# Attention: the 64-row rests of projections, v and output groups as two 32-row matmuls beside the logits

## Chip, cores and metric

The kernel runs on one core of a Trainium2 chip. The metric is the device time of one execution in microseconds, and the median of several runs is compared. Three runs of the kernel before took 1173.2, 1173.43 and 1175.64 us. A profile shows one execution: what each engine (PE, its weight loads PEld, DVE, ACT, POOL, and SP, which issues DMAs) did at which time.

## Reference

Four layers over x of 2048 rows and 576 columns: attention, gated MLP, attention, gated MLP, each added to its input. Cut to the attention, which the change touches:

```python
def _A_ref(x, wqkv, wo):
    B, S, D = x.shape                 # 1, 2048, 576
    H = 32; Dh = D // H               # 18
    W, dil = (8, 2)                   # each row looks at itself and 7 earlier rows, two apart
    qkv = (x @ wqkv).reshape(B, S, 3, H, Dh).transpose(2, 0, 3, 1, 4)
    q, k, v = (qkv[0], qkv[1], qkv[2])
    ...
    logits = jnp.einsum('bhsd,bhswd->bhsw', q, kg) * Dh ** (-0.5)
    logits = jnp.where(mask[None, None, :, :], logits, -1000000000.0)
    attn = _softmax(logits, axis=-1)
    o = jnp.einsum('bhsw,bhswd->bhsd', attn, vg)
    return o.transpose(0, 2, 1, 3).reshape(B, S, D) @ wo
...
x = x + _A_ref(_layernorm(x, axis=-1), A_wqkv, A_wo)
x = x + _B_ref(_layernorm(x, axis=-1), B_w_in, B_w_sp, B_b_sp, B_w_out)
```

The last two lines run twice.

## The kernel before

The layers are numbered 0 to 3; 0 and 2 are attention (`layer_A`), 1 and 3 the MLP. Rows are stored with even rows first, so that the dilated window becomes a band of eight neighbours. The normalized input stands transposed in `xnT`: 576 columns are five chunks of 128 rows, and the fifth holds 64 real rows; its other half meets weights that are zero (`zero_right`, L290). Every group that contracts over 576 columns is therefore five matmuls, c = 0 to 4, each over 128 rows:

- `PG(d, qk, cc)` (L402): one projection block of q or k, 512 columns, into a PSUM bank `pp`; `evac` copies it into a staging tile `stg`. When all parts of a staging tile are there, DMAs spread its heads, of 18 rows each, over `QK`, where each head has its own 32 rows; the queues of SP and POOL take them in turns.
- `VW(t, hh)` (L391): v for one key tile and half of the heads, 288 columns, into `v_ext`; `evac` is a copy on DVE or on ACT, by its last argument.
- `WO(i, hh)` (L523): half of an output tile, 288 columns; DVE adds the layer's input (L533).

The attention goes over 17 query tiles (t), two halves of the heads each, so over 34 steps s = 2t + hf (`NST`). `L_mm(s)` (L444) makes the logits of a step: 16 matmuls over 32 rows, a head per row tile of PE. The row tiles are 0 to 3 (j in the code). The pair jp = 0 uses row tiles 0 and 1, the pair jp = 1 uses 2 and 3, and each pair writes its own PSUM tile of two banks (`H_tile`, two of them, so a step's tiles are free again when the exponentials of the step before have read them). `EXP(s)` (L458) has ACT take the exponential of the two tiles, `PV(s)` (L468) multiplies with v in 16 matmuls into `O_ps`, and DVE divides (L482, L483). Four further PSUM banks (`PT_tile`) go round among O_ps, projections, v and output groups.

The order of the work on all engines is written out by hand (`manual_schedule`, L363); each engine runs its own instructions in program order. The loop at L762 does for each step s: `L_mm(s + 1)`, `EXP(s + 1)`, `PV(s)`, and then what `table` lists for s:

- projections: twelve `PG`, one in each of steps 1 to 12 in layer 0, in twelve of steps 0 to 12 in layer 2;
- v groups: one in most steps from 14 in layer 0 and from 3 in layer 2, up to step 29; from step 14 on every second one is evacuated by ACT, in layer 2 all of those before;
- output groups from step 8, one in a step, two in step 18;
- the normalization of finished output tiles: `LN_STATS` (DVE, then epsilon and power on POOL, L231 and L232), a step later `LN_XN` (POOL, L252 and L255) and the store `XST` (SP), later `XN_ST` and `LN_T`; loads `XO` of the layer's input (SP).

The rows from 1024 on of `QK` come from the projections of these steps; the logits of step 16 are the first to read them, and those of step 17 the first to read what the last two blocks (d = 3, d = 4) bring.

```python
for s in range(NST):
    if s + 1 < NST:
        L_mm(s + 1)
        EXP(s + 1)
    PV(s)
    for f, a in table.pop(s, []):
        f(*a)
```

Of the kernel before, what the change touches and what calls it, by code (L numbers as in the profile page):

```python
# [18 lines left out]
P = 128  # L19
# [44 lines left out]
class K:  # L64
# [267 lines left out]
    def layer_A(self, li):  # L332
# [57 lines left out]

        def VW(t, hh, dve):  # L391
            nk = tdim(t)[0]
            pv = self.PT_tile([P, 512], f32, "pv")
            for c in range(5):
                nc.tensor.matmul(pv[:nk, 0:288], lhsT=self.xnT[:, c, k0_(t):k0_(t) + nk],  # L395
                                 rhs=wv_sb[:, c, hh * 288:(hh + 1) * 288], start=(c == 0), stop=(c == 4))
            evac(v_ext[:nk, t, 16 * hh:16 * hh + 16, 0:DH], pv[:nk, 0:288].rearrange("p (b d) -> p b d", d=DH), dve)
# [4 lines left out]
        def PG(d, qk, cc, dve, queues=(nc.sync, nc.gpsimd)):  # L402
# [11 lines left out]
            pp = self.PT_tile([P, 512], f32, "pp")  # L414
            w0 = d * P + (640 if qk else 0)
            for c in range(5):
                w = wqk[:, c, w0:w0 + P] if c < 4 else wqk4[:, w0:w0 + P]
                nc.tensor.matmul(pp[:, :], lhsT=w, rhs=self.xnT[:, c, cc * 512:(cc + 1) * 512],  # L418
                                 start=(c == 0), stop=(c == 4))
# [21 lines left out]
        NST = 2 * NT  # L441
        L_tiles = {}

        def L_mm(s):  # L444
            t, hf = divmod(s, 2)
            nk, nq = tdim(t)
            L_tiles[s] = [self.H_tile("L_ps") for _ in range(2)]
            for jp in range(2):
                for ftl in range(4):
                    g = 4 * hf + ftl  # L450
                    for jj in range(2):
                        j = 2 * jp + jj
                        nc.tensor.matmul(L_tiles[s][jp][:nk, jj, ftl * P:ftl * P + nq],  # L453
                                         lhsT=kT[32 * j:32 * j + 32, g, k0_(t):k0_(t) + nk],
                                         rhs=qT[32 * j:32 * j + 32, g, q0_(t):q0_(t) + nq],
                                         start=True, stop=True, tile_position=(32 * j, 0))

        def EXP(s):  # L458
            nk, nq = tdim(s // 2)
            for jp, L_ps in enumerate(L_tiles.pop(s)):  # L460
                Lv = L_ps[:].rearrange("p a (b c) -> p a b c", c=P)
                nc.scalar.activation(out=P_bufs[(2 * s + jp) % 4][:nk, :, :, 0:nq], in_=Lv[:nk, :, :, 0:nq], func=ACT.Exp,  # L462
                                     scale=scale)
# [4 lines left out]
        def PV(s):  # L468
            t, hf = divmod(s, 2)
            nk, nq = tdim(t)  # L470
            O_ps = self.PT_tile([P, 512], f32, "O_ps")
            for jp in range(2):
                for ftl in range(4):
                    for jj in range(2):
                        idx = 4 * ftl + 2 * jp + jj
                        nc.tensor.matmul(O_ps[:, idx * (DH + 1):(idx + 1) * (DH + 1)],  # L476
                                         lhsT=P_bufs[(2 * s + jp) % 4][:nk, jj, ftl, :],
                                         rhs=v_ext[:nk, t, 16 * hf + idx, :], start=True, stop=True)
# [25 lines left out]
        def O_T(t):  # L504
            nq = tdim(t)[1]
            pt = self.PT_tile([P, 5, P], bf16, "pt")
# [16 lines left out]
        def WO(i, hh):  # L523
# [4 lines left out]
            pw = self.PT_tile([P, 512], f32, "pw")  # L528
            for c in range(5):
                nc.tensor.matmul(pw[:, 0:288], lhsT=oT[:, c, r0:r0 + P], rhs=wo_sb[:, c, hh * 288:(hh + 1) * 288],  # L530
                                 start=(c == 0), stop=(c == 4))
            hs = slice(hh * 288, (hh + 1) * 288)
            nc.vector.tensor_tensor(out=st["x"][:, hs], in0=pw[:, 0:288], in1=st["xo"][:, hs], op=ALU.add)  # L533
# [20 lines left out]
        if li == 0:  # L554
# [72 lines left out]
            VW(0, 0, False)  # L627
            VW(0, 1, False)
            VW(1, 0, False)
# [6 lines left out]
            VW(1, 1, False)  # L636
# [4 lines left out]
            VW(2, 0, False)  # L641
            VW(2, 1, False)
# [17 lines left out]
            for k_, (d, cc) in enumerate(order):  # L660
                for qk in ((1, 0) if d < 4 else (0,)):
                    PG(d, qk, cc, False, (nc.gpsimd, nc.sync) if d in (0, 4) else q2)
                if k_ == 3:
                    VW(3, 0, False)
                    VW(3, 1, False)
# [5 lines left out]
        else:  # L671
            for k_, (d, cc) in enumerate([(d, cc) for d in range(5) for cc in range(2)]):
                for qk in ((1, 0) if d < 4 else (0,)):
                    PG(d, qk, cc, k_ == 0, (nc.gpsimd, nc.sync) if d == 0 else q2)
# [10 lines left out]
        for t in range(nvw0, nvw - (1 if li == 0 else 0)):  # L685
            for hh in range(2):
                VW(t, hh, li == 0)
# [11 lines left out]
        def at(s, f, *a):  # L699
            table.setdefault(s, []).append((f, a))  # L700
        pgs = [(d, qk, cc) for d, cc in ((0, 2), (1, 2), (2, 2), (0, 3), (1, 3), (2, 3), (3, 2), (3, 3), (4, 2), (4, 3))
# [3 lines left out]
        for k_, (d, qk, cc) in enumerate(pgs):  # L705
            at(1 + k_ if li == 0 else (k_ * PG_END) // len(pgs), PG, d, qk, cc, True)
        vws = [(t, hh) for t in range(nvw, NT) for hh in range(2)]
        if li == 0:
            at(0, VW, *vws[0], True)
            at(13, VW, *vws[1], True)  # L710
# [4 lines left out]
        for k_, (t, hh) in enumerate(vws):  # L715
            assert vsteps[k_] <= 2 * t - 2 + hh
            at(vsteps[k_], VW, t, hh, vsteps[k_] >= PG_END and k_ % 2 == 0)
# [8 lines left out]
        for i in range(NS):  # L726
# [3 lines left out]
            at(s, WO, i, 0)  # L730
            at(s1, WO, i, 1)
# [20 lines left out]
        for k_, (d, qk, cc) in enumerate(pre):  # L752
# [3 lines left out]
            PG(d, qk, cc, li > 0 or k_ < 4, q2)  # L756
            if li == 0 and k_ == 3:
                self.fill_window_rows(QK, 1)
        if li == 0:
            VW(nvw - 1, 0, False)  # L760
            VW(nvw - 1, 1, False)
        for s in range(NST):  # L762
            if s + 1 < NST:
                L_mm(s + 1)
                EXP(s + 1)
            PV(s)
            for f, a in table.pop(s, []):
                f(*a)
        for s in sorted(table):
            for f, a in table[s]:  # L770
# [376 lines left out]
```

## Time and profile before

| what | us |
|---|---|
| runs | 1173.2, 1173.43, 1175.64 |
| the profiled execution | 1174.15, its span 1172.3 |
| PE matmuls busy | 1156.2 (99% of the span) |
| first burst of logits in layer 0, in layer 2 | at 42.90, at 614.14 |
| last burst in layer 0, in layer 2 | at 120.07, at 698.03 |
| exponentials (L462) | 136, 972 ns each |
| projection matmuls (L418) | 379 ns each, 128x512 |
| v and output matmuls (L395, L530) | 285 and 286 ns each, 128x288 |
| logit matmuls (L453) | 213 ns each, 32 rows x 120 columns |
| copies of v on ACT (L389), on DVE (L387) | 405 and 452 ns each |
| LN_XN on POOL (L252) | 2307 ns each |

A matmul's duration contains the time through the array; matmuls overlap, so what a matmul costs PE is read from the distance of two starts. In a timeline line, the first number is the start in the span, the second how long the merged instructions last, "x16" how many they are; what stands in brackets is idle time of the engine before it and what ended it. "SPq" and POOL lines with DMA_DIRECT2D are issues of DMAs, not their transfers.

### The profile page before, as it was taken

Reading aid. Unit: us, or ns where it says so; the run is one execution under the profiler, and the core shown is the slowest. Engines: PE = TensorE matmul, PEld = TensorE weight load, DVE = VectorE, ACT = ScalarE, POOL = GpSimd, SP = SyncE. Lnnn points to the kernel's source line nnn. Section 1 sums busy time; section 2 is a strip of 40 time slices with the busy share of each in tenths; the row PEclk is TensorE's granted clock in tenths of the full one; section 3 lists DMA queues with packets and bytes.
Section 4 is the critical chain, followed back from the end, with each engine's and each line's share of the span. In section 5 each row is a group of like instructions: output and inputs, shape, how many; then the busy total and the mean of one; then the engine's idle time right before and its main releaser. Section 6 shows DMA issues by size and latency. Waiting matters only on the chain.

```text
span 1172.3 us, 19950 instructions
## 1 busy us (share of the span) xinstructions
PE 1156.2 (99%) x8161; PEld 618.8 (53%) x8258; DVE 552.6 (47%) x1137; ACT 339.5 (29%) x491; POOL 280.4 (24%) x412
## 2 busy tenths in 40 slices
PE   9999999999999999999999999999999999999998
PEld 5567544444444444457755774444444444444677
DVE  8678788333223322235545786863332223322321
ACT  5578555011110111102256884541011110111000
POOL 3769855000000000002153897540000000000000
DMA  8799895000000000059547797940000000001332
GB/s 197 192 172 246 185 230 114 23 12 12 12 11 2 12 12 1 18 170 277 159 98 115 204 236 194 236 85 1 12 12 12 12 12 1 12 1 46 110 106 74
DMA packets 182800, 106.44 MB, mean 91 GB/s; under 512 B 134938, under 2 KB 164042, under 8 KB 182709
## 3 DMA queue, kind: packets, MB, share of 16 engines
q1 hardware_dynamic: 170117, 84.54, 31.6%
q0 software_dynamic: 6240, 14.88, 4.6%
q10 hardware_dynamic: 6352, 5.75, 1.6%
q8 instruction: 64, 1.05, 0.4%
q14 instruction: 27, 0.22, 0.1%
HBM read 42.40 MB, written 21.77 MB: 55 GB/s over the span
## 4 chain that ended last, share of the span: by engine, by line
PE 94%; DMA 2%; issue 1%; ACT 1%; DVE 1%; POOL 1%; SPq 0%; DVEq 0%; ACTq 0%
PE pg L986 42%; PE po L1035 12%; PE pz L962 6%; PE pz1s L962 6%; PE pzs L838 6%; PE pz L838 6%; PE pp L418 5%; PE pw L530 3%; PE pv L395 3%; PE L_ps L453 3%; PE O_ps L476 2%; DMA wqk_sb<-in_A_wqkv_dram 1%; ACT P_sb L462 1%; DMA QK<-stg 1%; POOL QK L78 1%
## 5 line engine op out<-in xcount | busy, mean ns | idle before, releaser
L986 PE MATMUL pg<-Wq,Z 128*128 128x512 bf16 x2256 | 497.7, 379 | 2.5
L986 PEld LDWEIGHTS <-Z 128*128 128x128 bf16 x2304 | 225.4, 98 | 271.9
L990 DVE TENSOR_TENSOR g_tmp<-pg,ln_xn 128x512 f32<-128x512 f32 x144 | 99.7, 692 | 421.5 <-PE pg L986 421.5
L981 ACT ACTIVATE z1T<-pz 128x1024 bf16<-128x1024 f32 x36 | 34.9, 1021 | 500.2 <-PE pz L962 500.2
L78 POOL DMA_DIRECT2D wout<-in_B_w_out_dram x4 | 4.3, 1080 | 598.8 <-PE pg L986 598.8
L1035 PE MATMUL po<-wout,Z 128*128 128x288 bf16 x1152 | 141.4, 286 | 0.0
L462 ACT ACTIVATE P_sb<-L_ps 128x960 bf16<-128x960 f32 (+1 forms) x136 | 124.6, 972 | 32.7 <-PE L_ps L453 31.5
L1035 PEld LDWEIGHTS <-Z 128*128 128x128 bf16 x1152 | 112.7, 98 | 28.8
L838 PEld LDWEIGHTS <-xnT 128*128 128x128 bf16 (+1 forms) x800 | 68.0, 97 | 76.4 <-issue 11.5
L991 DVE TENSOR_TENSOR Z<-g_tmp,z1T 128x512 bf16<-128x512 f32 x144 | 99.7, 692 | 12.2
L887 DVE BATCH_NORM_STATS2 z_st<-zp 128x6 f32<-128x512 bf16 (+1 forms) x160 | 91.2, 617 | 10.7 <-ACT zp L885 10.5
L962 PEld LDWEIGHTS <-w 128*128 128x128 bf16 (+1 forms) x640 | 53.7, 97 | 74.0 <-issue 13.6
L418 PE MATMUL pp<-xnT,wqk_sb 128*128 128x512 bf16 x341 | 81.4, 379 | 1.5 <-DMA wqk_sb<-in_A_wqkv_dram 0.5
L252 POOL TENSOR_SCALAR ln_xn<-x_new,ln_mv,ln_rstd 128x576 bf16<-128x576 f32 x32 | 73.8, 2307 | 2.3
L1045 DVE TENSOR_TENSOR x_new<-po,xo 128x288 f32<-128x288 f32 (+1 forms) x64 | 28.8, 456 | 87.4 <-PE po L1035 83.4
L962 PE MATMUL pz<-xnT,w 128*128 128x512 bf16 (+1 forms) x314 | 66.2, 380 | 0.3
L962 PE MATMUL pz1s<-xnT,w 128*128 128x512 bf16 (+1 forms) x314 | 65.9, 379 | 0.5 <-issue 0.3
L838 PE MATMUL pzs<-win2a,xnT 128*128 128x512 bf16 (+1 forms) x234 | 58.6, 358 | 0.7 <-DVE x_new L533 0.4
L838 PE MATMUL pz<-win2a,xnT 128*128 128x512 bf16 (+1 forms) x234 | 58.5, 357 | 0.3
L78 POOL DMA_DIRECT2D QK<-stg x80 | 48.4, 610 | 38.3 <-DVE stg L387 18.2
L911 POOL TENSOR_SCALAR Z<-zp,z_mv,z_rstd 128x256 bf16<-128x256 bf16 x32 | 54.6, 1706 | 3.3
L885 ACT ACTIVATE zp<-pz 128x1024 bf16<-128x1024 f32 (+2 forms) x56 | 36.6, 720 | 61.7 <-PE pz L838 61.7
(108 smaller groups left out, 950.7 us busy)
## 6 DMA issues: line engine op xcount, KB each, us to landing
xres<-x_new SPq DMA_DIRECT2D x48, 288.0 KB
xo<-xres SPq DMA_DIRECT2D x32, 288.0 KB
wout<-in_B_w_out_dram POOLq DMA_DIRECT2D x4, 1296.0 KB, 7.7
xn_rows<-ln_xn SPq DMA_DIRECT2D x32, 160.0 KB
xo<-xres SPq DMA_DIRECT2D x8, 576.0 KB
w<-in_B_w_in_dram SPq DMA_DIRECT2D x16, 256.0 KB
QK<-stg POOLq DMA_DIRECT2D x52, 72.0 KB, 4.2
QK<-stg SPq DMA_DIRECT2D x42, 72.0 KB
```

What stands on the lines that cost most here:

```text
L78: return eng.dma_start(out=out, in_=in_)
L252: e.tensor_scalar(out=xn[:nrows, 0:D], in0=x_t[:nrows, :], scalar1=mv[:nrows, 0:1], scalar2=rstd[:nrows, 0:1], op0=ALU.subtract, op1=ALU.mult)
L418: nc.tensor.matmul(pp[:, :], lhsT=w, rhs=self.xnT[:, c, cc * 512:(cc + 1) * 512], start=(c == 0), stop=(c == 4))
L462: nc.scalar.activation(out=P_bufs[(2 * s + jp) % 4][:nk, :, :, 0:nq], in_=Lv[:nk, :, :, 0:nq], func=ACT.Exp, scale=scale)
L838: nc.tensor.matmul(out[:, o0:o0 + n], lhsT=self.xnT[r0:r1, c, r * P:(r + 1) * P], rhs=win2(c)[r0:r1, w0:w0 + n], start=start, stop=stop, t ...
L887: nc.vector.bn_stats(out=st[:, x // 512, :], in_=zp[:, x:x + min(512, w0 + n - x)])
L911: eng.tensor_scalar(out=Z[:, b0:b1, i, :], in0=zv[:, b0:b1, :], scalar1=mv[:, 0:1], scalar2=rstd[:, 0:1], op0=ALU.subtract, op1=ALU.mult)
L962: nc.tensor.matmul(outs[a_], lhsT=w1[r0:r1, c, sub * P:(sub + 1) * P], rhs=self.xnT[r0:r1, c, q * 512:(q + 1) * 512], start=start, stop=st ...
L986: nc.tensor.matmul(pg[:, :], lhsT=Z[:, jj, i, sub * P:(sub + 1) * P], rhs=Wq[q][:, i, :], start=(i == 0), stop=(i == NS - 1))
L990: nc.vector.tensor_tensor(out=tmp[:], in0=pg[:, :], in1=bsp[:, qs], op=ALU.add)
L991: nc.vector.tensor_tensor(out=uT(jj)[:, sub, qs], in0=tmp[:], in1=z1Ts[jj, sub][:, qs], op=ALU.mult)
L1035: nc.tensor.matmul(acc[hh], lhsT=u_rows(j, i), rhs=wouts[j // NJH][:, j % NJH, hh * 288:(hh + 1) * 288], start=(j == 0), stop=(j == NJ - 1))
```

## The change

A group becomes a `Unit`. `plain()` does the five matmuls as before. A unit that is listed `early` is spread over two bursts of logits instead: `begin()` multiplies the first 32 of the 64 rest rows in row tile 0, at the head of the burst that precedes the unit's step; `middle()` does the four full chunks in the unit's place in the step; `end()` multiplies the other 32 rows in row tile 1 between the two halves of the next burst; `done()` evacuates right after the first of the two exponentials of that burst. One unit in each of steps 0 to 31 of both layers is early, 64 in all; a second or third unit of a step stays plain. The pairs of row tiles of the logits become (1, 2) and (0, 3). The four PSUM banks are allocated once and handed out by `take` by a written-down guess of when each is free; a begun unit holds its bank until it is done.

```diff
+        NST = 2 * NT
+        banks, free, held, now = [], [0.0] * 4, set(), [-1]
+        tails_w = []
+        JP = ((1, 2), (0, 3))
+
+        def take(name, rel=0.0):
+            if now[0] < 0:
+                return self.PT_tile([P, 512], f32, name), None
+            k_ = min((x for x in range(4) if x not in held), key=lambda x: free[x])
+            if rel is None:
+                held.add(k_)
+            else:
+                free[k_] = now[0] + rel
+            return banks[k_], k_
+
+        def mm(out, lr, start, stop, rg=None):
+            kw = {} if rg is None else dict(tile_position=(32 * rg, 0))
+            return nc.tensor.matmul(out, lhsT=lr[0], rhs=lr[1], start=start, stop=stop, **kw)
+
+        class Unit:
...
+            def plain(u):
+                ps, _ = take(u.name, 1.25)
+                for c in range(5):
+                    mm(ps[:, 0:u.n], u.op(c), c == 0, c == 4)
+                u.fin(ps)
+
+            def done(u):
+                held.discard(u.k)
+                free[u.k] = now[0] + u.rel
+                u.fin(u.ps)
+
+            def begin(u):
+                u.ps, u.k = take(u.name, None)
+                mm(u.ps[:, 0:u.n], u.op(4, 0, 32), True, False, 0)
+
+            def middle(u):
+                for c in range(4):
+                    mm(u.ps[:, 0:u.n], u.op(c), False, False)
+                tails_w.append(u)
+
+            def end(u):
+                mm(u.ps[:, 0:u.n], u.op(4, 32, 64), False, True, 1)
+
         def VW(t, hh, dve):
...
+            return Unit("pv", 288, lambda c, r0=0, r1=P: (self.xnT[r0:r1, c, k0:k0 + P], wv_sb[r0:r1, c, ws]),
+                         lambda ps: evac(v_ext[:, t, 16 * hh:16 * hh + 16, 0:DH],
+                                         ps[:, 0:288].rearrange("p (b d) -> p b d", d=DH), dve), 0.45 if dve else 0.9)
...
-        def L_mm(s):
+        def L_mm(s, begins=()):
...
+            ends = tails_w[:]
+            tails_w.clear()
             for jp in range(2):
+                if jp == 0:
+                    for u in begins:
+                        u.begin()
+                else:
+                    for u in ends:
+                        u.end()
                 for ftl in range(4):
                     g = 4 * hf + ftl
                     for jj in range(2):
-                        j = 2 * jp + jj
+                        j = JP[jp][jj]
...
+            return ends
+
+        def EXP(s, jps=(0, 1)):
...
-            O_ps = self.PT_tile([P, 512], f32, "O_ps")
+            O_ps = take("O_ps", 0.8)[0]
...
+        def early(s, f, *a):
+            if s > NST - 3 or s in begins:
+                at(s, plain, f, *a)
+                return
+            begins[s] = (f, a)
+            at(s, lambda: begins.pop(s).middle())
+            return True
+
...
-            at(1 + k_ if li == 0 else (k_ * PG_END) // len(pgs), PG, d, qk, cc, True)
+            early(1 + k_ if li == 0 else (k_ * PG_END) // len(pgs), PG, d, qk, cc, True)
...
-            at(vsteps[k_], VW, t, hh, vsteps[k_] >= PG_END and k_ % 2 == 0)
+            early(vsteps[k_], VW, t, hh, vsteps[k_] >= PG_END and k_ % 2 == 0)
...
-            at(s, WO, i, 0)
-            at(s1, WO, i, 1)
+            e0 = early(s, WO, i, 0)
+            if early(s1, WO, i, 1) or e0 and s1 == s:
+                s1 += 1
...
+        banks.extend(self.PT_tile([P, 512], f32, "bank") for _ in range(4))
         for s in range(NST):
+            now[0] = s
+            if s in begins:
+                f, a = begins[s]
+                begins[s] = f(*a)
             if s + 1 < NST:
-                L_mm(s + 1)
-                EXP(s + 1)
+                fins = L_mm(s + 1, [begins[s]] if s in begins else [])
+                EXP(s + 1, (0,))
+                for u in fins:
+                    u.done()
+                EXP(s + 1, (1,))
             PV(s)
             for f, a in table.pop(s, []):
                 f(*a)
```

Since the DMAs of a staging tile are issued when its last part is evacuated, those of the projections of steps 10 and 12 now come, in POOL's order, behind the `LN_XN` that the table lists for the same step, and in SP's order behind that step's `XST` and `XO`.

## The prediction

> **What bounds the kernel now.** I read the page first, then the timeline of the attention layers, then POOL alone. The page says where to look:
>
> ```profile
> PE 1156.2 (99%) x8161; PEld 618.8 (53%) x8258; DVE 552.6 (47%) x1137; ACT 339.5 (29%) x491; POOL 280.4 (24%) x412
> PE 94%; DMA 2%; issue 1%; ACT 1%; DVE 1%; POOL 1%; SPq 0%; DVEq 0%; ACTq 0%
> ```
>
> PE sets the end, so only what PE loses or gains counts. The change touches the two attention loops alone (L(1) at 48.9 to about 123 us, and 621.4 to about 701). I call the sixteen logit matmuls that L_mm(n) issues burst n. Three bursts of the first layer:
>
> ```profile
> 50.50 0.39 PE L453 MATMUL L_ps<-QK 32*128 32x120 bf16 x8
> ...
> 51.42 0.38 PE L453 MATMUL L_ps<-QK 32*128 32x120 bf16 x8 [0.53 <-ACT P_sb L462]
> ...
> 53.33 0.41 PE L453 MATMUL L_ps<-QK 32*128 32x120 bf16 x16
> 53.67 0.56 PE L476 MATMUL O_ps<-v_ext,P_sb 128*128 128x19 bf16 x16
> 54.08 1.24 PE L418 MATMUL pp<-xnT,wqk_sb 128*128 128x512 bf16 x5
> 55.26 0.82 PE L453 MATMUL L_ps<-QK 32*128 32x120 bf16 x16
> ```
>
> Eight matmuls (two row tiles) last 0.39; sixteen last 0.41 where nothing holds them, and PV starts 0.34 after the first. So a free burst already runs in all four row tiles side by side. Only where the second half waits for ACT, as at 51.42 or 55.26 (0.82 long), do two tiles stand empty. The later steps (v group and output group) show what decides that:
>
> ```profile
> 101.25 0.41 ACT L389 CAST v_ext<-pv 128x288 bf16<-128x288 f32 x1
> 101.28 0.52 PE L453 MATMUL L_ps<-QK 32*128 32x120 bf16 x16
> 101.76 1.83 ACT L462 ACTIVATE P_sb<-L_ps 128x960 bf16<-128x960 f32 x2
> 103.46 0.57 PE L453 MATMUL L_ps<-QK 32*128 32x120 bf16 x16
> 103.94 1.83 ACT L462 ACTIVATE P_sb<-L_ps 128x960 bf16<-128x960 f32 x2 [0.35 <-PE L_ps L453]
> ```
>
> The exponentials start 0.48 after a burst, last 1.83, and the next burst's second half follows 0.06 later (55.64 to 55.70). With T the time from burst to burst, the second half is late by j = 2.37 - T. A burst then takes j + 0.315 to PV. After it come PV 0.42, the groups (projection 1.08, v or output 0.61 each, from the starts of their first matmuls) and 0.09 before the next burst. Where j decides, two steps together take 2.37 + 0.315 + 0.42 + 0.09 + groups: 4.28 for projections (57.60 to 61.88 shows 4.28), 4.41 for v plus output (101.28 to 105.70 shows 4.42). Where PE never waits, a step is 0.34 + 0.42 + 0.09 + groups: projection plus output 2.54, as the trace has from 69.02 on. Carried burst by burst, these rules give 70.7 from burst 1 to burst 33; the trace has 71.2.
>
> **The removed matmul.** Each of 64 groups (24 projections; 33 v and 7 output groups) loses a full fifth matmul: 0.215 for 512 columns (1.08/5), 0.122 for 288. If all of it came back: 24 x 0.215 + 40 x 0.122 = 10.0 us.
>
> **The two added ones.** A 32-row matmul streams as many columns as the full one, so it holds its row tile just as long. No row shows one beside the logits; the nearest is the free burst, where four tiles stream at once. I take that it runs beside the others. Row tile 0 then has the begin plus four logits, row tile 1 four logits plus an end: a burst lasts at least 0.315 + 0.213 = 0.53 with 512 columns, 0.435 with 288. So a step in which PE never waited gets 0.19 (0.095) back on the burst and gains only 0.025: 2.54 becomes 2.515. Where ACT holds the second half, j covers the addition and a pair of steps gains the whole matmul: projections 4.28 to 4.06, v plus output 4.41 to 4.295. The other bound, the 32-row matmul beside nothing, adds its columns to each burst twice a step: by the same rules 10.2 us more over both layers. The lower bound, no growth of the burst at all, is 2.5 less.
>
> By the Trainium skill (TensorE: Matmul & The Clock Gate, "The mechanism") matmuls start and end strictly in program order. Here the trace disagrees: in program order the second eight would come after the first, and sixteen could not last 0.41 where eight last 0.39; by that rule the tiles would be idle in every burst and the gain nearer to the lower bound just given. The skill's TensorEngine Tiling (Array Packing), "Key Properties", has PE drain when the tile mode changes; the 0.09 agrees, and it would add nothing, since begin and end stand inside the burst.
>
> **The cast that moves.** A delayed group is evacuated one step later, between the two exponentials of the next burst. Projections go to DVE, which has room there (DVE 83% busy from 79 to 114 us). But 17 early v groups are cast by ACT (steps 15, 17, 20, 22, 24, 26, 28 of the first layer; 6, 13, 14, 16, 19, 21, 23, 25, 27, 29 of the other). Before, the cast ran after both exponentials, as at 101.25, in ACT's 0.35 of spare time. Now the second exponential waits for it: 0.86 + 0.40 instead of 0.86 after the first. Queued behind it is the second half of the next burst, and behind that, in PE's order, all of PE. j becomes 2.77 - T, and a pair of steps takes 4.695 where it took 4.41: +0.28 per cast, against -0.12 without.
>
> Carried burst by burst, before to after: first layer, bursts 1-9 -0.85, 9-14 -0.14, 14-18 -0.24, 18-30 +1.57, to the end +0.28: sum +0.6. Third layer: -0.69, -0.14, +0.17, +1.07, and +0.93 at the end, where a step holds little but the late cast: sum +1.3. Without the moved cast it would be -2.1 and -1.8. Bounds of the cast: 0 (then -5.8) and 0.45 (+0.8).
>
> **The queues that move.** With a projection's evacuation its QK DMAs leave one step later, and so behind the POOL work of the step. POOL before, in the first layer:
>
> ```profile
> 74.22 0.59 POOL L232 TENSOR_TENSOR ln_rstd<-ln_rstd,neg_half 128x1 f32<-128x1 f32 x1
> 75.28 2.41 POOL L78 DMA_DIRECT2D QK<-stg  x4 [0.48 <-DVE stg L387]
> 77.75 2.31 POOL L252 TENSOR_SCALAR ln_xn<-x_new,ln_mv,ln_rstd 128x576 bf16<-128x576 f32 x1
> 80.12 0.24 POOL L255 COPY ln_xn<-ln_xn 128x64 bf16<-128x64 bf16 x1
> ...
> 80.64 0.57 POOL L232 TENSOR_TENSOR ln_rstd<-ln_rstd,neg_half 128x1 f32<-128x1 f32 x1
> 81.18 2.21 POOL L78 DMA_DIRECT2D QK<-stg  x4
> ```
>
> The last four issues (81.18) carry rows that burst 17 reads, at 85.76; the trace's landing records end at 85.35, so 0.4 is spare. In the new order LN_XN of tile 0 and then of tile 1 run ahead of the two QK groups. From the end of the first power at 74.81 less about 0.7 that PE is ahead: LN_XN and copy 2.6, QK 2.45, epsilon and power 0.95, LN_XN and copy 2.65, then the last four QK issues, starting at 82.8 and ending at 85.0 instead of 83.39; landing is 1.96 behind as before, at 87.0. Burst 17, itself 0.9 earlier (84.9), would read its last rows at about 85.1 and waits to 87.0: 1.9, of which the rules leave +2.3 in the sum (the next steps lose some of what they had won). Bounds: 0 if POOL is as early as before, 3 if tile 0's normalization is no earlier at all. SP passes two xres stores and one xo load (0.44 + 0.47 + 0.42) ahead of its QK issues and ends near 84.5, less late than POOL. In the third layer the same four issues go from 656.28 to about 658.7 and land near 662.8, against burst 17 at 662.97 less 0.55: +0.2.
>
> Costed at nothing: PSUM banks (an output group's bank is read until 104.22 and its next group starts at 104.99; 0.77 of cover, and what exceeds it falls on PE in each step) and POOL's total (33.4 of 35.3 us busy from 79 to 114; it would bind a faster loop, but this one is not).
>
> **Sum.** 0.6 + 1.3 + 2.3 + 0.2 = +4.4 us on the profiled execution's 1174.15 (span 1172.3). The median of the runs is 0.7 lower, 1173.43, so the forecast is 1177.8.
>
> **Rivals.**
> 1. ACT absorbs the cast. Place: steps 15 to 29; price -5.8; it decides if the second exponential ends by the time PE has its second half to issue, that is if the cast costs the pair under 0.1. For: ACT is 12% idle there. Against: the idle time lies before the first exponential, not between the two. 1172.0, not slower. Chance 0.12.
> 2. The QK rows are in time: -2.5, 1175.3. For: LN_XN of tile 0 could start early. Against: 0.4 of slack and two LN_XN of 2.3 ahead. Chance 0.18. Together with rival 1: -3.9, 1169.5, chance 0.10.
> 3. The tiles are free in every burst (the change does all it says on PE): -2.5 with the other delays, 1175.3. Against: 0.41 beside 0.39. Chance 0.07.
> 4. The 32-row matmuls stand alone: +10.2, 1188. Against: the same rows. Chance 0.08.
> 5. The forecast, 1176 to 1181: 0.45.
>
> A measurement of this kernel tells 0.2% (2.35 us) from no change. Slower: the forecast, rival 4, and about half of rivals 2 and 3: 0.65. Same: the rest of those and most of rival 1: 0.21. Faster: rivals 1 and 2 together and a little of 1: 0.14. The range, 1170.5 to 1183, leaves out rival 4 and the far end of the joint case; the forecast alone has 1175 to 1181.
>
> **What would show it.** In the new trace: a free projection-plus-output step still near 2.5, with a burst of about 0.53 to PV; 0.4 of cast between the two exponentials and second halves of bursts late by some 0.7 in every other step from 15 on; in the first layer a wait of 1 to 2.5 us for a QK DMA at burst 17. I am wrong if free steps fall to 2.35 or less, if the pairs with casts take 4.4 or less, or if burst 17 does not wait.

## The result and the profile after

The changed kernel is slower. In the first comparison its time stood to that of the kernel before as 1.0048 (95% interval 1.003 to 1.0067); in the second, r1 below, the medians were 1181.09 us (1178.41 to 1182.32, 6 runs) and 1174.95 (19 runs), ratio 1.005 (1.0034 to 1.0067). One of the six executions of the changed kernel in the first comparison took 1989.95 us at a mean granted TensorE clock of 0.556 and is left out of the ratio. The profile after is that of an execution of r1: 1180.76 us, span 1179.0. Its page, the lines of busy time and of the chain that ended last:

```profile
span 1179.0 us, 20122 instructions
PE 1159.1 (98%) x8225; PEld 620.5 (53%) x8322; DVE 553.3 (47%) x1137; ACT 339.4 (29%) x491; POOL 282.6 (24%) x412
PE 92%; DVE 2%; DMA 1%; issue 1%; ACT 1%; POOL 1%; SPq 1%; DVEq 0%; ACTq 0%
```

PE has 64 matmuls more, two for one in 64 groups, and its share of the chain fell from 94% to 92%: waits have come in. The helper `mm` records the matmuls of all groups, so projections, v and output groups are all L408 now, and their tile is `bank`; logits are L506, exponentials L517, PV L531. Where the time lies is read from the starts of the bursts of logits (us between two starts, layer 0 and layer 2; the last column is what the prediction's rules give for the stretch):

| stretch of bursts | before | after | change | forecast |
|---|---|---|---|---|
| layer 0: 1 to 9 | 17.24 | 16.58 | -0.66 | -0.85 |
| 9 to 14 | 13.04 | 12.89 | -0.15 | -0.14 |
| 14 to 18 | 8.84 | 10.15 | +1.31 | -0.24 + 2.3 |
| 18 to 30 | 26.51 | 27.56 | +1.05 | +1.57 |
| 30 to 33 | 5.53 | 6.71 | +1.18 | +0.28 |
| layer 2: 1 to 9 | 19.21 | 18.66 | -0.55 | -0.69 |
| 9 to 14 | 15.78 | 15.87 | +0.09 | -0.14 |
| 14 to 18 | 8.84 | 10.28 | +1.44 | +0.17 + 0.2 |
| 18 to 30 | 26.64 | 27.12 | +0.48 | +1.07 |
| 30 to 33 | 6.15 | 6.55 | +0.40 | +0.93 |
| both layers | | | +4.6 | +4.4 |

The two profiled spans differ by 6.6. Of the other 2.0, 2.56 lie ahead of the first burst (42.90 and 45.46), where the change touches nothing: in the profiled executions of the kernel before and of r1 to r12 that burst starts between 41.66 and 45.46. The two latest starts, r1's and r8's (44.28), are the two with a stretch of 3.41 us at half clock shortly ahead of it, at 40.07 and at 38.47; what brought it on there is not shown. The rest, -0.5, lies in the way from layer 2's first burst to its second (7.27 to 6.94) and in the MLP layers.

The losses are in steps where PE waits or runs at half clock, as the lines show. First a burst in which nothing waits, in the timeline of r1:

```profile
70.87 0.38 PE L408 MATMUL bank<-xnT,wqk_sb 32*128 32x512 bf16 x1
70.87 0.40 PE L506 MATMUL L_ps<-QK 32*128 32x120 bf16 x11
...
71.09 0.37 PE L408 MATMUL bank<-xnT,wqk_sb 32*128 32x512 bf16 x1
71.09 0.37 PE L506 MATMUL L_ps<-QK 32*128 32x120 bf16 x5
...
71.40 0.56 PE L531 MATMUL bank<-v_ext,P_sb 128*128 128x19 bf16 x16
...
73.38 0.38 PE L408 MATMUL bank<-xnT,wqk_sb 32*128 32x512 bf16 x1
```

The two 32-row matmuls do run beside the logits, and they stretch the burst: PV starts 0.53 after the start of the burst (0.34 before), and the next burst 2.51 after it (2.54 before). What the groups lost with their fifth matmul came back in the burst. Next a pair of steps with a cast of v on ACT, in layer 2:

```profile
684.00 2.73 ACT L517 ACTIVATE P_sb<-L_ps 128x960 bf16<-128x960 f32 x3
...
684.42 0.38 PE L506 MATMUL L_ps<-QK 32*128 32x120 bf16 x8
...
685.04 0.39 PE L506 MATMUL L_ps<-QK 32*128 32x120 bf16 x8
...
687.46 0.97 ACT L517 ACTIVATE P_sb<-L_ps 128x960 bf16<-128x960 f32 x1 [0.72 <-PE L_ps L506]
...
688.33 0.40 ACT L389 CAST v_ext<-bank 128x288 bf16<-128x288 f32 x1
...
688.60 0.99 ACT L517 ACTIVATE P_sb<-L_ps 128x960 bf16<-128x960 f32 x1
```

The cast at 688.33 stands between the two exponentials of a burst. From the start of the first to that of the second it is 1.14 (687.46 to 688.60) where it was 0.86, and ACT idles 0.72 before the first, where it has nothing to do. The cast of the pair before (at 683.72) shows what follows: the second half of the next burst comes 0.62 after the first (684.42 to 685.04). The pair takes 4.60 (684.42 to 689.02) for 4.42 before. Last the place where q and k of the last blocks are due, with POOL, SP and PE of layer 0:

```profile
82.55 2.31 POOL L252 TENSOR_SCALAR ln_xn<-x_new,ln_mv,ln_rstd 128x576 bf16<-128x576 f32 x1
84.92 0.24 POOL L255 COPY ln_xn<-ln_xn 128x64 bf16<-128x64 bf16 x1
85.45 2.19 POOL L78 DMA_DIRECT2D QK<-stg  x4 [0.29 <-DVE rec L537]
...
83.24 0.42 SPq L78 DMA_DIRECT2D xo<-in_A_x_dram  x1
83.75 3.10 SPq L78 DMA_DIRECT2D QK<-stg  x4
...
87.52 0.33 PE L506 MATMUL L_ps<-QK 32*128 32x120 bf16 x6
88.09 0.21 PE L506 MATMUL L_ps<-QK 32*128 32x120 bf16 x1 [0.25 <-DMA QK<-stg]
...
89.33 0.21 PE L506 MATMUL L_ps<-QK 32*128 32x120 bf16 x1 [0.36 <-DMA QK<-stg]
```

`LN_XN` and its copy run ahead of the last four issues on POOL, which end at 87.64 (83.39 before). Burst 17 starts at 87.52 and its last matmul at 89.33, 0.05 after the last of these DMAs landed (89.28 in the trace's landing records). T, the time from this burst to the next, is 3.57 instead of 2.26.

### The profile page after: what moved, and what is told of

Read it like the earlier page. It is cut to its first block, busy times and chain, and to the rows that moved or that the text cites. A ratio compares the mean times of both kernels' runs of the same rounds, so it can differ in the third digit from the quotient of the medians.

```text
span 1988.2 us, 20219 instructions
## 1 busy us (share of the span) xinstructions
PE 1982.1 (100%) x8322; PEld 802.3 (40%) x8322; DVE 561.3 (28%) x1137; ACT 346.5 (17%) x491; POOL 278.1 (14%) x412
## 4 chain that ended last, share of the span: by engine, by line
PE 99%; DVE 0%; ACT 0%; issue 0%; ACTq 0%
PE pg L1064 45%; PE po L1113 13%; PE bank L408 8%; PE pz L916 6%; PE pz1s L1040 6%; PE pz L1040 6%; PE pzs L916 6%; PE pp L408 5%; PE bank L531 2%; PE L_ps L506 2%; PE pv L408 1%; DVE ln_st L644 0%; PE bank L563 0%; ACT P_sb L517 0%; PE pt L664 0%
## 5 line engine op out<-in xcount | busy, mean ns | idle before, releaser
L1064 PE MATMUL pg<-Wq,Z 128*128 128x512 bf16 x2304 | 888.6, 583 | 0.0
L1064 PEld LDWEIGHTS <-Z 128*128 128x128 bf16 x2304 | 307.6, 133 | 578.9 <-issue 578.9
L1113 PE MATMUL po<-wout,Z 128*128 128x288 bf16 x1152 | 249.4, 413 | 0.0
L1113 PEld LDWEIGHTS <-Z 128*128 128x128 bf16 x1152 | 152.5, 132 | 97.1 <-issue 1.0
L517 ACT ACTIVATE P_sb<-L_ps 128x960 bf16<-128x960 f32 (+1 forms) x136 | 126.9, 975 | 83.2 <-PE L_ps L506 81.3
L1040 PE MATMUL pz1s<-xnT,w 128*128 128x512 bf16 (+1 forms) x320 | 114.0, 575 | 0.0
L1040 PE MATMUL pz<-xnT,w 128*128 128x512 bf16 (+1 forms) x320 | 114.0, 571 | 0.0
L916 PE MATMUL pz<-win2a,xnT 128*128 128x512 bf16 (+1 forms) x240 | 98.8, 538 | 0.0
L916 PE MATMUL pzs<-win2a,xnT 128*128 128x512 bf16 (+1 forms) x240 | 97.8, 539 | 0.0
L408 PE MATMUL pp<-xnT,wqk_sb 128*128 128x512 bf16 x240 | 93.3, 581 | 0.0
L408 PEld LDWEIGHTS <-wqk_sb 128*128 128x128 bf16 (+1 forms) x384 | 47.8, 129 | 80.4 <-issue 77.0
L408 PE MATMUL bank<-wo_sb,oT 128*128 128x288 bf16 (+1 forms) x327 | 80.1, 380 | 0.0
L916 PE MATMUL pzs<-win2b,xnT 64*128 64x512 bf16 (+3 forms) x160 | 64.0, 544 | 0.0
```

The lines of the kernel that those rows point to most:

```text
L408: return nc.tensor.matmul(out, lhsT=lr[0], rhs=lr[1], start=start, stop=stop, **kw)
L916: nc.tensor.matmul(out[:, o0:o0 + n], lhsT=self.xnT[r0:r1, c, r * P:(r + 1) * P], rhs=win2(c)[r0:r1, w0:w0 + n], start=start, stop=stop, t ...
L1040: nc.tensor.matmul(outs[a_], lhsT=w1[r0:r1, c, sub * P:(sub + 1) * P], rhs=self.xnT[r0:r1, c, q * 512:(q + 1) * 512], start=start, stop=st ...
L1064: nc.tensor.matmul(pg[:, :], lhsT=Z[:, jj, i, sub * P:(sub + 1) * P], rhs=Wq[q][:, i, :], start=(i == 0), stop=(i == NS - 1))
L1113: nc.tensor.matmul(acc[hh], lhsT=u_rows(j, i), rhs=wouts[j // NJH][:, j % NJH, hh * 288:(hh + 1) * 288], start=(j == 0), stop=(j == NJ - 1))
```

## The experiments

Every kernel was run beside the kernel before on the same chip: r1 to r4 on one, r5 to r8 on a second, r9 to r12 on a third. Medians in us; ratio to the kernel before with its 95% interval (an estimate from all runs, not the ratio of the two medians); "full clock" counts the runs whose mean granted TensorE clock is given as 1.000.

| run | median | before | ratio | mean clock | full clock |
|---|---|---|---|---|---|
| r1, the change | 1181.09 | 1174.95 | 1.005 (1.0034 to 1.0067) | 0.9977 | 0 of 6 |
| r2, cast last | 1179.17 | 1174.95 | 1.0027 (1.0012 to 1.0042) | 0.9971 | 0 of 8 |
| r3, POOL's order restored | 1180.13 | 1174.95 | 1.0041 (1.0025 to 1.0057) | 0.9978 | 2 of 6 |
| r4, both | 1177.97 | 1174.95 | 1.003 (1.0014 to 1.0046) | 0.9973 | 1 of 12 |
| r5, both queues restored | 1176.07 | 1173.67 | 1.0022 (1.0007 to 1.0038) | 0.9986 | 5 of 12 |
| r6, r5 and cast last | 1175.9 | 1173.67 | 1.0014 (1.0002 to 1.0026) | 0.9982 | 4 of 12 |
| r7, r6 and a plain tail | 1175.5 | 1173.67 | 1.0003 (0.9983 to 1.0024) | 0.9991 | 8 of 12 |
| r8, projections alone | 1174.72 | 1173.67 | 1.001 (0.9993 to 1.0027) | 0.9986 | 4 of 12 |
| r9, before, outputs later | 1174.17 | 1173.92 | 1.0 (0.9987 to 1.0012) | 0.9994 | 7 of 11 |
| r10, r8, outputs later | 1177.3 | 1173.92 | 1.002 (1.0004 to 1.0035) | 0.9983 | 3 of 12 |
| r11, r7, outputs later | 1178.15 | 1173.92 | 1.0029 (1.0015 to 1.0043) | 0.9973 | 0 of 12 |
| r12, r8 in layer 2 alone | 1172.98 | 1173.92 | 0.9991 (0.9976 to 1.0006) | 0.9995 | 6 of 11 |

The kernel before had 10 of 19, 20 of 35 and 24 of 35 runs at full clock.

### r1: the change as it is

> The changed kernel once more, for a profile of an execution at full clock. The forecast's theory: 1177 to 1182 us; in the trace, free steps with a projection and an output group near 2.51 us with about 0.53 us from the first logit matmul to PV; from step 15 on second halves of bursts late by about 0.7 us after a cast between two exponentials; burst 17 of the first layer waiting 1 to 2.5 us for a QK DMA. Rival (clock): the loss is PE running at a lower granted clock for part of the span (0.996 to 0.999 mean instead of 1.000); then the attention loops last no longer than before and the loss lies elsewhere.

Measured: the table and the lines above. The loops last 4.6 longer, with the waits that the forecast named, so the clock is not the whole of the loss; about 1.0 of it is (below, under the clock).

### r2: ACT's cast after both exponentials

```diff
                 EXP(s + 1, (0,))
                 for u in fins:
-                    u.done()
+                    if u.rel != 0.9:
+                        u.done()
                 EXP(s + 1, (1,))
+                for u in fins:
+                    if u.rel == 0.9:
+                        u.done()
```

A unit that ACT evacuates has rel 0.9; DVE's stay where they were.

> The changed kernel with ACT's copies of delayed v groups after both exponentials instead of between them; DVE's stay between. The forecast's theory (the late copy delays the next burst's second half): 5.8 us less than the changed kernel, about 1175 us, pairs of v-plus-output steps at 4.30 us instead of 4.70. Rival 1 (ACT absorbs the copy): no change against the changed kernel, within 1 us. Rival (clock): no change either.

ACT in the timeline of r2, at the same place of layer 2:

```profile
683.02 1.83 ACT L517 ACTIVATE P_sb<-L_ps 128x960 bf16<-128x960 f32 x2 [0.41 <-PE L_ps L506]
684.74 0.41 ACT L389 CAST v_ext<-bank 128x288 bf16<-128x288 f32 x1
685.08 1.83 ACT L517 ACTIVATE P_sb<-L_ps 128x960 bf16<-128x960 f32 x2
```

The exponentials are together again (1.83 for two), and the cast takes ACT's spare time before the next pair. Most pairs of steps take 4.30 to 4.32 now, less than the 4.42 before the change. Bursts 18 to 30 took 26.60 and 26.12, against 27.56 and 27.12 in r1: -0.96 and -1.0. So the place of the cast was all but 0.09 of layer 0's loss in that stretch, and in layer 2 all of it and some more. The wait at burst 17 stayed (T 4.09 and 3.42). The gain is less than expected: the two loops together are 3.2 shorter than r1's, not 5.8, and the median is 1.9 under r1's; the two intervals overlap.

### r3: LN_XN a step later, so that POOL issues QK first

```diff
-            at(s1 + 1, LN_XN, i)
+            at(s1 + 2 if s1 + 1 <= 12 else s1 + 1, LN_XN, i)
```

> The changed kernel with LN_XN of output tiles 0 and 1 listed one step later, so that POOL issues the QK DMAs of the last projections ahead of them, in the order of the kernel before. The forecast's theory: burst 17 of the first layer no longer waits, 2.5 us less than the changed kernel, about 1178 us. Rival 2 (the rows were in time): no change, within 0.5 us.

In layer 2 the wait at burst 17 shrank (T 2.52, in r1 3.42). In layer 0 it did not. POOL, SP and PE in the timeline of r3:

```profile
80.95 2.21 POOL L78 DMA_DIRECT2D QK<-stg  x4
...
80.64 1.58 SPq L78 DMA_DIRECT2D xo<-in_A_x_dram  x1
82.31 3.10 SPq L78 DMA_DIRECT2D QK<-stg  x4
...
84.73 0.33 PE L506 MATMUL L_ps<-QK 32*128 32x120 bf16 x6
86.02 0.40 PE L506 MATMUL L_ps<-QK 32*128 32x120 bf16 x2 [0.96 <-DMA QK<-stg]
```

POOL is done issuing at 83.16, as before the change. SP, behind two stores and a load of xo that took 1.58 to issue, ends at 85.41, and burst 17 waits as long (T 3.87). Its last matmul starts at 86.84, when POOL's last rows have been there since 85.61 (landing record), so it waits for SP's: SP's queue alone can hold the burst. No run makes POOL alone late. The median is 1.0 under r1's, where 2.5 was expected, and the intervals overlap. This execution has a second loss: bursts 18 to 30 took 30.72, 4.2 over before, with a wait of 2.1 of DVE for a load of `xo`, a wait of 2.0 of PE behind it, and 3.41 us at half clock from 98.93.

### r4: both

The edits of r2 and r3 together.

> Both edits, ACT's copies last and the QK DMAs ahead. The forecast's theory: -2.1 and -1.8 us for the two layers against the kernel before, so about 1169.5 us, ratio 0.997. If the clock or the row tiles alone make the loss, it stays at the changed kernel's time, about 1180.

The casts' stretch is as in r2 (26.69 and 26.24), and burst 17 still waits: PV starts 2.21 and 1.96 after it, for 1.95 and 1.80 in r1. T is 4.88 and 3.58, but in layer 0 about 1.0 of it is a stretch at half clock from 88.23 (from PV to the next burst 2.67, in r1 1.62). In both layers the long wait ends 0.04 after a DMA of POOL's has landed (87.23 and 87.27, 667.38 and 667.42), although POOL issues in the old order again: these DMAs took 4.1 to 6.0 us to land, for 1.9 to 3.1 in the kernel before. About 1169.5 was expected; the median is 1177.97, still 3.0 over before. What is left as in r1 is SP's order, with a store and a load of `xo` ahead of the QK issues.

### r5 and r6: no early projection in steps 10 and 12

```diff
-            if s > NST - 3 or s in begins:
+            if s > NST - 3 or s in begins or s in (10, 12):
```

The groups of these steps are plain again, so their evacuation and their QK DMAs stand where they stood in both queues; r6 has the edit of r2 too.

> The changed kernel with all groups of steps 10 and 12 plain, so that the last QK DMAs are issued where the kernel before issues them, on POOL and on SP. Theory (both queues held burst 17; with POOL's order alone restored SP still issued its last four 1 to 2 us late): burst 17 waits for ACT only, PV under 0.7 us after its start in both layers; 1.3 + 1.2 us less than the changed kernel in the loops, about 1178. Rival (the DMAs themselves are slow, whoever issues them): burst 17 still waits over 1 us.

> The same with ACT's copies after both exponentials. Theory: no wait at burst 17 and v-plus-output pairs at 4.32 us; loops shorter than the kernel before by about 1 us (first layer) and 2 us (third); about 1172 if nothing else changed. Rival (clock): stretches of 3.41 us at half the granted clock remain at the end of the attention loops, each worth up to 1.7 us, and keep it at 1174 or more.

The wait is gone but for 0.4 in r6's layer 0: T at burst 17 is 2.27 and 2.16 in r5, 2.62 and 2.17 in r6, for 2.26 before. In layer 0 a stall ahead of burst 17, told next, may have helped; r8, which has the same queues and hardly a stall, has 2.31 in both layers. So the order of the two queues made the wait, and POOL's order alone did not. About 1178 was expected of r5, which came in below it (1176.07), and about 1172 of r6, which did not reach it (1175.9). The profiled executions show a new wait, earlier in layer 0. Bursts 11, 12 and 13 of r5 took 6.48, 4.36 and 2.81 for 2.54 each before. Who waited for whom in r5 from 69 to 82 us (total, times, longest):

```profile
DVE oT L557 <- DMA o_slot<-o_t: 4.7, 1, 4.7
PEld L408 <- DVE oT L557: 2.9, 1, 2.9
PE bank L408 <- DVE x_new L585: 2.8, 1, 2.8
```

The transposes of the second finished attention tile (SP issued them at 64.86 in r5, at 66.06 before) have not landed at 69.2, when DVE is to copy them into `oT`. Behind that copy stand the addition of an output group and the evacuation of a projection, and behind those PE. Before, the same copy waited 0.4. Part of the length of bursts 12 and 13 is the clock: PE ran at half clock for 6.83 us from 73.90.

### r7: and the last steps plain

```diff
-            if s > NST - 3 or s in begins:
+            if s > NST - 3 or s in begins or s in (10, 12) or s > 27:
```

With the edit of r2 too.

> The same with the groups of steps 28 to 31 plain too. Theory of the clock: with full matmuls in the tail PE is as active as in the kernel before, no half-clock stretch at the end of the loops, 1 to 3 us less than the run without this edit. Rival (the half-clock stretches have nothing to do with the change): as many of them, and a time within 0.5 us.

The end of layer 0's loop is as before (5.54 for 5.53). The median is 0.4 under r6's, not 1 to 3, so the gain that was expected of the plain tail is not shown. It is 1.8 over before, and the interval includes no change. The profiled execution has the stall of r5 at its worst (8.39, 4.36, 3.16 for bursts 11 to 13), with half clock from 73.77 to 84.01. DVE and PE in its timeline:

```profile
68.48 0.46 DVE L585 TENSOR_TENSOR x_new<-bank,xo 128x288 f32<-128x288 f32 x1 [1.64 <-DMA xo<-in_A_x_dram]
...
76.04 0.34 DVE L557 COPY oT<-o_slot 128x600 bf16<-128x600 bf16 x1 [5.85 <-DMA o_slot<-o_t]
...
76.80 1.36 PE L408 MATMUL bank<-wo_sb,oT 128*128 128x288 bf16 x5 [4.68 <-DVE x_new L585]
```

A load of `xo` is late as well, by 1.64, so more than one transfer is behind. The busy time by stretches of 5 us (PE, PEld, DVE, ACT, POOL, then granted clock, share of the DMA engines, GB/s), the kernel before and then r7:

```profile
57.00:62.00 5.00, 4.95 (x82) 2.61 (x84) 3.17 (x7) 4.39 (x6) 2.77 (x6) 1.00 1.21 196
62.00:67.00 5.00, 4.95 (x96) 2.88 (x93) 3.51 (x7) 4.20 (x6) 2.67 (x6) 1.00 0.93 179
67.00:72.00 5.00, 4.95 (x86) 3.00 (x84) 3.19 (x7) 3.29 (x4) 0.83 (x2) 1.00 0.98 144
```

```profile
62.00:67.00 5.00, 4.93 (x82) 2.81 (x82) 3.35 (x8) 4.51 (x5) 2.75 (x5) 1.00 1.14 188
67.00:72.00 5.00, 4.93 (x84) 2.88 (x83) 1.68 (x4) 3.41 (x4) 0.00 (x0) 1.00 1.21 137
72.00:77.00 5.00, 0.32 (x3) 0.21 (x3) 0.96 (x3) 0.25 (x1) 0.00 (x0) 0.68 1.09 164
```

The share of the DMA engines was 0.93 to 1.21 in this stretch before the change, with PE at 99%. This suggests that layer 0 stands near two limits at once, and that what PE gains brings it nearer to transfers that come no sooner. It is not shown. The executions of r5, r6 and r7 also began their loop 0.8 to 1.2 sooner than the one of before (burst 1 at 47.79, 48.08 and 47.67 for 48.91), which is more than the 0.66 that PE gains up to burst 9. And r2, with burst 1 at 48.23 and the same gain, has no stall: its copy starts at 70.01 after a wait of 0.38.

### r8: projections alone

```diff
-            if s > NST - 3 or s in begins:
+            if s > NST - 3 or s in begins or s in (10, 12) or f is not PG:
```

v and output groups are plain throughout.

> Only projections are early (steps 1 to 9 and 11), v and output groups all plain: no ACT copy is delayed. Theory: the early steps keep their gain (bursts 1 to 9: -0.66 and -0.56 us against the kernel before, 9 to 14 about -0.1 each), the v-plus-output steps are as before (pairs 4.42); about 1.3 us less than the kernel before. Rival (every spread group costs something): not faster than the kernel before.

Bursts 1 to 9 keep their gain (16.58 and 18.66, as in r1), 18 to 30 are as before (26.53 in both layers), 9 to 14 a little longer (13.31 and 16.13 for 13.04 and 15.78). The profiled execution has loops 0.4 and 0.5 shorter than before (70.79 for 71.16, 76.10 for 76.62). The median is not less: 1174.72, ratio 1.001 (0.9993 to 1.0027), nor is it at full clock alone (1174.11 of 4 runs for 1173.57 of 20). No moved cast, queue or tail is left here that could take the gain. In the profiled execution 1.38 goes ahead of the first burst (44.28 for 42.90), where the two kernels do not differ; what took the gain in the other runs, one trace does not show.

### r9 to r11: layer 0's second output tile two steps later

If late transposes take the gain in layer 0, giving them more time should return it.

```diff
-        units = [x for x in range(lag, NST) for _ in range(2 if x in twice else 1)]
+        units = [x for x in range(lag, NST) for _ in range(0 if li == 0 and x in (10, 11) else
+                 2 if x in twice or li == 0 and x in (12, 13) else 1)]
...
-                at(min(2 * t + 6, s), O_CP, t)
+                at(min(2 * t + (7 if t == 2 else 6), s), O_CP, t)
```

> The kernel before, with layer 0's second output tile two steps later (output groups of steps 10 and 11 go to 12 and 13, and the copy from o_slot for t = 2 is issued a step later). Theory D (in layer 0 the transposes of finished attention tiles land late behind the spreading of q and k, at 72 to 76 us in every execution whatever PE does, so an earlier PE only waits): before had a wait of 0.4 us there in its profiled execution and gains at most that; two steps without an output group cost about 4.27 - 2 x 2.54 + (6.3 - 2 x 2.54) = +0.4 us. So 0 to +0.4 us against before, and the wait before the copy into oT near 72 us is gone. Rival N (the stall of 2.9 to 5.8 us in three profiled executions is a matter of the execution, not of the place): 0 to +0.4 us as well. This run is the base for the next two.

> r8 (projections alone ahead, queues as before) with layer 0's second output tile two steps later as in r9. Theory D: the 0.66 us that the projections of layer 0 gain are kept now, and so is layer 2's 0.56: 1.0 to 1.4 us faster than r9, and no wait of over 1 us for o_slot near 72 us. Rival N (projections gain in their steps, and something else of the kernel, the clock or the spread of executions, takes it): within 0.5 us of r9, as r8 was of before (ratio 1.001).

> r7 (queues as before, ACT's copies last, plain from step 28 on) with layer 0's second output tile two steps later as in r9. Theory D: the stall of r7's profiled execution (bursts 11 to 13 took 8.39, 4.36 and 3.17 us for 2.52 each) is gone or under 1 us; steps 14 to 27 cost 4.31 a pair for 4.42 in six to seven pairs of a layer, so 0.6 us a layer less than r10: 1.5 to 2.5 us faster than r9, about 1171.5 to 1172.5, under the kernel before. Rival N: within 0.7 us of r9. Half-clock stretches of up to 1.7 us each can take 1 to 3 us of it under either.

The median of r9 is 0.25 over before, in the range expected, though its interval includes no change; its profiled execution has no wait for `o_slot`. The other two missed: r10 was 3.1 slower than r9, r11 4.0. The remedy failed, and that late transposes take the gain is not shown by it. In r10, from 72 to 81 us, another instruction waits for the same transposes:

```profile
DVE o_t L538 <- DMA o_slot<-o_t: 2.5, 1, 2.5
```

The division of a later tile writes the buffer from which the transposes still read, 9.1 after SP began to issue them (66.50 to 75.62). Burst 13 took 4.20 (3.15 in r9), and later burst 17 waited again (T 3.35). In this execution, shifting the reader by two steps moved the wait to the next user of the buffer. In r11's profiled execution, the quickest here with r12's (span 1171.1), the loops took 70.72 and 76.26, under r9's 72.06 and 76.62; but the median of its 12 runs is 1178.15, and none of them had the full clock. What these runs lost, the one trace does not show.

### r12: projections ahead in layer 2 alone

```diff
-            if s > NST - 3 or s in begins:
+            if s > NST - 3 or s in begins or s in (10, 12) or f is not PG or li == 0:
```

> r8 with the projections ahead in layer 2 alone; layer 0 runs as in the kernel before. Theory D: layer 2 keeps its 0.56 to 0.85 us and layer 0 has no more waits than before: 0.5 to 0.9 us faster than before, ratio 0.9993 to 0.9996. Rival N: as r8, 0 to 1 us slower than before.

0.94 under before in the median (1172.98 for 1173.92), 0.77 at full clock (1172.87 of 6 runs for 1173.64 of 24); the ratio, 0.9991 (0.9976 to 1.0006), does not exclude no change. It is the best of the kernels here, and the only one with its median under before's. Its layer 2 is r8's to 0.02 (76.10), its layer 0 the one of before (71.18). That r12 is under before and r8 is not would fit a layer 0 that cannot take the gain; as each interval holds the other's ratio, it does not show it.

### The clock

The runs differ in one thing more. Two stretches of r1 around the end of layer 0's loop, and the same place in the kernel before (columns as above; the clock is the third number from the end):

```profile
118.50:121.90 3.40, 2.72 (x69) 1.86 (x68) 2.51 (x9) 2.83 (x5) 2.75 (x5) 1.00 0.74 224
121.90:125.40 3.50, 3.50 (x56) 2.03 (x54) 2.05 (x6) 2.70 (x4) 1.89 (x2) 0.51 0.74 180
```

```profile
114.00:117.40 3.40, 2.99 (x65) 2.03 (x64) 2.84 (x10) 3.29 (x5) 3.15 (x5) 1.00 0.90 230
117.40:120.90 3.50, 3.24 (x74) 2.27 (x70) 2.91 (x10) 3.25 (x5) 3.25 (x5) 1.00 0.93 140
```

After 3.4 us in which PE was 80% busy (2.72 of 3.40) TensorE ran at half clock for 3.41 us; before, PE was 88% busy there (2.99) and kept its clock. The edit of r3 does not reach the end of that loop, and r3, without a drop there, took 5.72 from burst 30 to 33 for r1's 6.71: such a stretch cost about 1.0, as much as the one behind the wait of r4. r1's execution has three (at 40.07, 121.99 and 705.67); the profiled executions of before, r9 and r12 have none. So a wait can cost more than its length, but need not: r2 and r3 waited as long as r4 at burst 17 of layer 0 and kept the clock.

## Why the prediction was right, point by point

**The sum.** +4.4 was forecast on the profile and +4.6 came between bursts 1 and 33 of the two layers. The runs say +5.6 to +5.9 (0.48 to 0.5%), with an interval from 3.5 to 7.9. That the sum is met so closely is in part luck: its terms have errors up to 1.1 that cancel, the table gives each, and about 1.0 of the +4.6 is a stretch at half clock for which the prediction has no term.

**The removed and the added matmuls.** Right as to mechanism: a free burst is 0.53 to PV and its step 2.51, as forecast (0.53, 2.515). A pair of projection steps whose second half waits for ACT is 4.12, forecast 4.06; the gain in bursts 1 to 9 is 0.66 and 0.55 for 0.85 and 0.69. Rivals 3 and 4 (tiles free in every burst, or 32-row matmuls that stand alone) are excluded by these lines: the step gains 0.03, not 0.215, and loses nothing.

**The cast that moves.** Right, and mis-sized by a third: "0.86 + 0.40 instead of 0.86" is 1.14, since the second exponential starts 0.27 after the cast does, before the cast's end (688.33 + 0.40 against 688.60). The pair is 4.60 instead of 4.695, and 18 to 30 cost 1.05 and 0.48 for 1.57 and 1.07. r2 takes that loss away by moving the cast alone, so it is the cast's; rival 1 (ACT absorbs the cast) needs another place for it in the program.

**The queues.** In layer 0 the forecast holds: POOL's last issue was to end 0.1 after the start of burst 17 and ended 0.12 after it, and the rows landed 1.76 after it for 2.1. The wait is 1.42 (PV 1.95 after the burst for 0.53), forecast 1.9, and bursts 14 to 18 cost +1.31 where the sum has -0.24 + 2.3.

In layer 2 the term of +0.2 failed: T is 3.42 for 2.26, +1.16. The step that failed is that the rows "land near 662.8", 1.96 after the end of POOL's issues as in layer 0. POOL's first issue of the four came sooner than forecast, 4.46 ahead of burst 17 for 3.7, but the landing took 5 us where it took 2 before. The place before and in r1, from all that touches `QK` there, and PE in r1:

```profile
L78 POOL DMA_DIRECT2D QK<-stg x4: 505/524/668, 656.3 to 658.0; - x4
DMA to landing us min/median/max: 1.9/2.1/3.1
```

```profile
L78 POOL DMA_DIRECT2D QK<-stg x4: 507/526/647, 663.2 to 664.9; - x4
DMA to landing us min/median/max: 4.7/5.0/5.5
668.96 0.41 PE L506 MATMUL L_ps<-QK 32*128 32x120 bf16 x2 [0.94 <-DMA QK<-stg]
```

The matmul at 668.96 starts 0.04 after one of these four landed (668.92). In layer 2 of r1 to r4, where SP issues a store and a load of `xo` ahead of its QK DMAs, POOL's take 3.8 to 6.0 us to land, in r3 and r4 too, where POOL's own order is restored; in r5 to r8, with both queues as before, 1.9 to 3.0. So SP's order goes with the landing of POOL's rows, and the prediction asked of SP only how late its own rows are ("less late than POOL"). Which transfer slows them was not isolated, and in layer 0 of r1, with the same order on SP, they took 1.9 to 2.2. Rival 2 (the rows are in time) is out in both layers.

**The end.** +0.28 and +0.93 for the late cast; measured +1.18 and +0.40. In layer 0 about 1.0 of it is the half clock, on which the prediction has no term. Without it (r3) it was +0.19.

**What was costed at nothing.** The cover of the banks nearly held (in r1 PE waited for a bank twice in layer 0's loop, 0.6 in all), and POOL's total did. Missing from the list was the DMA engines' share: 0.93 to 1.21 in layer 0 while PE was 99% busy. In r1 the copy into `oT` waited 0.5 there, so it did not touch this forecast. With the cast and the queues mended (r6, r7) the kernel comes within 0.2% of before and not 3.9 us under it, as rivals 1 and 2 together gave. The profiled executions of r5 to r7 lose the gain of layer 0 in the stall. In layer 2, which has no such stall, r6's loop is 0.63 shorter and not 1.8, with 0.43 lost in bursts 9 to 14; why is not shown.

**What stays open.** What makes the QK rows of layer 2 land late in r1 to r4; what makes the same transposes land 5 us after their issue in one execution and 10 in another, and so whether layer 0 is at a second limit; which level of activity brings the half clock; and whether r12 is faster at all.

## What to carry to other kernels

Packing a matmul into idle row tiles gains only where they are idle because something else holds the second half; in a burst that already runs four tiles wide it comes back as a longer burst. An edit that delays an evacuation delays everything that is issued with it: place a copy where its engine idles, not in the middle of a pair that others wait for, and walk through every queue that issues for the same tile, with what now stands ahead of it, not only the one that looks latest. A landing time read in one order of the queues (2 us here) need not hold in another (5 us). Before speeding up one engine in a stage, look at the share of the DMA engines in that stage: PE at 99% does not exclude a second limit close by.

## What the runs showed of the hardware

TensorE fell to half clock for 3.41 us at a time (6.83 in r5 and 10.24 in r7 are two and three times that), in stages where PE was not idle but some 80% busy (r1: 2.72 of 3.40 before the drop at 121.99) or stalled (r4: 1.82 of 3.20 before the drop at 88.23). The Trainium skill, TensorE: Matmul & The Clock Gate, "Part 1: The HAM clock gate", gives a window of 3413 ns and half rate after an idle one; the length and the rate agree with these traces, but "idle" does not describe what stood before r1's drop. None of r1's 6 runs, r2's 8 and r11's 12 had the full clock in the mean, while 54 of 89 of the kernel before had it.

ACT starts an exponential 0.27 after the start of a cast that lasts 0.40 (688.33, 688.60): what such an instruction costs between two others is read from the distance of starts, not from its duration.

The same four DMAs of POOL's took 1.9 to 3.1 us from issue to landing in the kernel before and 4.7 to 5.5 in r1 (layer 2).
